# Splitting the first loads by even and odd phases, with direct products ahead of the odd ones, and longer DMA tails in a kernel's own scheduler

## The chip, the cores and the metric

The kernel runs on one core of a Trainium2 chip. The metric is the device time in microseconds (us) of one execution. A profile's span is about 1.8 us shorter than the time of the same execution. Differences between spans are used below to locate time, and differences between timed runs to judge it. Every run quoted here was classed as fast, so no slow run enters a comparison.

Names: TensorE does matmuls and transposes, VectorE and ScalarE do the elementwise work, GpSimd does little here but issue accumulating DMAs, and the sync engine's queue issues nearly all other DMAs.

## The reference, cut to what matters

```python
# B=2, T=4000, D=512, K=5 taps, U=8; all bf16
xp = pad(x, 2)                                     # x (2, 4000, 512)
h  = sum(xp[:, i:i+T, :] @ w1[i] for i in range(5))
h  = gelu(h)[:, ::2, :]                            # stride 2
f  = sum(pad(h, 2)[:, i:i+T1, :] @ w2[i] for i in range(5))
f  = gelu(f)[:, ::2, :]
fe, ge = f @ w_f, g @ w_g
out = tanh(fe[:, :, None, :] + ge[:, None, :, :]) @ w_o   # (2, 1000, 8, 512)
```

## The kernel before

The kernel computes each convolution partly with *direct* products (tap times sample, one output column block) and partly with *transformed* products. In the latter, sums of samples (tiles `xt`) meet sums of taps (tiles `w_t`, `w_b`), so fewer matmuls are needed. The price is work on VectorE, which makes those sums.

A Python object `Plan` records every operation and orders each engine's instructions with a small cost model. In the head, from the first load to the first block of products, the order is pinned to the order of the source on all four engines. After that only TensorE is pinned, and the model decides on the other engines. An engine then runs its instructions in the order that was written.

The part of the model that the change touches tells when a DMA issued by GpSimd is believed to have landed:

```python
HOP = 0.16                                  # us between engines
...
if o.dma and e == "pool":
    soft = max(soft, end + 1.0)
    busy = wire > soft + 1.0
    soft += o.nbytes / (60e3 if busy else 230e3)
    wire += o.nbytes / 220e3 if busy else 0.0
    end = max(soft, end + 2.0)
```

The head loads two pieces of 512 KB (128 partitions with four consecutive samples each, so all four phases), then five taps of `w1` with 512 KB each. It transposes the samples on TensorE, and makes sums:

```python
NWARM = 10
...
def load_xr(rt):                            # all four phases of one piece
    dst = xr[rt][:].map(lambda a: a.rearrange("p r k c -> p (r k c)"))
    src = x[1, 4*P*rt:4*P*(rt+1), :].rearrange("(p r) c -> p (r c)", r=4)
    return pl.dma("sp", lambda e: e.dma_start(dst.ap, src), (), (dst,))
...
came = [load_xr(rt) for rt in range(2)]
came.append(load_w1(0))
for i in (1, 3, 4, 2):
    came.append(load_w1(i, came[-3]))       # issued only when came[-3] has landed
...
warm_mm(NWARM)                              # matmuls of zeros
for pp in range(2):                         # 0: even phases, 1: odd phases
    for rt in range(2):
        ...                                 # 8 transposes on TensorE, then
        if pp: act(o, pv, ACT.Copy)         # eviction on ScalarE
        else:  ...tensor_copy...            # or on VectorE
...
for w in ("b1", "a3"):
    t0.shift(w)                             # ScalarE
for w in ("a0", "a1", "a2", "b3", "b1", "a3"):
    t0.xf(w)                                # VectorE: sums of samples
w1sum13(); w1sums(2, "s"); w1sums(1, "s")   # VectorE: sums of taps
direct(0)                                   # 8 products of the tap w1[0]
filt3("a0")                                 # 12 products
direct(1); direct(3); filt3("b1"); direct(4); filt3("b3", "a3"); direct(2)
pl.pin = ("pe",)
```

## Time and profile before

| | before |
|---|---|
| time, median (range) of 3 runs | 269.05 us (268.66 to 269.43) |
| span of the profiled run | 267.6 us |
| first useful product starts | 7.51 us |
| TensorE's longest wait after its start | 1.64 us, at 57.6 us |

The page's first part for the kernel before gives each engine's busy time, share of the span and instruction count.

```profile
PE 260.0 (97%) x1582; PEld 151.8 (57%) x1582; DVE 201.1 (75%) x362; ACT 181.2 (68%) x302; POOL 6.9 (3%) x20
```

TensorE (PE) is nearly always busy, so a change can gain only by removing TensorE work, by closing its few gaps, or by letting useful products begin sooner. The busy share hides one thing: the first 7.5 us count as busy, but they are zero matmuls and transposes.

This is TensorE's timeline of the kernel before. The columns are start in us, length in us, engine, source line, operation, output and inputs, shapes and count. The bracket gives the idle time before the group and what ended it.

```profile
1.19 4.12 PE L417 MATMUL acc<-zero 128*128 128x512 bf16 x10 [1.19 <-DVE zero L424]
5.15 2.21 PE L510 MATMUL acc<-ident,xr 128*128 128x128 bf16 x32
7.51 1.02 PE L417 MATMUL acc<-xs,w_sb 128*128 128x252 bf16 x8 [0.15 <-issue]
8.37 1.45 PE L417 MATMUL acc<-xt,w_sb 128*128 128x252 bf16 x12
...
16.98 1.45 PE L417 MATMUL acc<-xs,w_t 128*128 128x252 bf16 x12
18.27 2.74 PE L417 MATMUL acc<-xt,w_t 128*128 128x252 bf16 x24
...
23.10 1.15 PE L417 MATMUL acc<-xs,w_t 128*128 128x252 bf16 x8 [0.36 <-issue]
...
59.20 0.60 PE L417 MATMUL acc<-wide,w_t 128*128 128x334 bf16 x3 [1.64 <-DVE wide L404]
```

The eight products at 7.51 are `direct(0)` and the twelve at 8.37 are `filt3("a0")`. The 24 at 18.27 use the summed taps `w_t` that VectorE makes. Starts are what to compare: 12 products from 8.37 to the next group at 9.66 are 1.29 us, 0.1075 us each. The wait at 59.20 is the second convolution's operand `wide`.

What feeds `wide` is visible in ScalarE's timeline of the kernel before (same columns):

```profile
51.07 1.06 ACT L409 ACTIVATE w_t<-half 128x1024 bf16<-128x1024 f32 x1 [1.57 <-DMA half<-w_t]
52.03 0.57 ACT L409 ACTIVATE hT<-acc 128x498 bf16<-128x498 f32 x1
...
54.13 1.06 ACT L409 ACTIVATE w_t<-half 128x1024 bf16<-128x1024 f32 x1 [1.01 <-DMA half<-w_t]
55.09 0.57 ACT L409 ACTIVATE hT<-acc 128x498 bf16<-128x498 f32 x1
```

Twice ScalarE stands and waits for an accumulating DMA into `half` (1.57 and 1.01 us), and an `hT` eviction, from which `wide` is made, stands behind it in the same queue. The model believed that those DMAs had landed already.

The sync queue's timeline of the kernel before shows the loads of the head (start, length of the issuing stretch, waits included):

```profile
0.74 0.87 SPq L440 DMA_DIRECT2D xr<-in_x_dram  x2
1.66 7.63 SPq L435 DMA_DIRECT2D w_sb<-in_w_dram  x5
```

Two whole pieces take 0.87 us to issue, 0.43 us each. The first tap goes out at 1.66. In the table by stretches (start and end, length, busy us of PE, PEld, DVE, ACT and POOL with counts, clock, DMA share, GB/s), the wire is full:

```profile
7.50:10.00 2.50, 2.49 (x24) 2.26 (x25) 2.19 (x5) 2.47 (x4) 0.00 (x0) 1.00 1.02 325
```

### The profile page before, as it was taken

To read this page: it belongs to the slowest core of one execution; us is meant where nothing else is said; L and a number is where in the kernel's file an instruction comes from. 1 tells how busy PE (TensorE), PEld (TensorE's weight loads), DVE (VectorE), ACT (ScalarE), POOL (GpSimd) and SP (SyncE) were. 2 spreads that over 40 slices of the span, in tenths; PEclk is the share of its full clock that TensorE was granted. 3 is DMA by queue.
4 is the path that set the end of the run, shared out by engine and by line. 5 is a ranking of instruction groups with operands and counts; after the bars stand their busy time and mean duration, and the time that the engine had idled before them with its cause. 6 is when DMAs were issued, how large, how long until landed. Compare 5 with 4: busy or idle time off the path is not lost.

```text
span 267.6 us, 4331 instructions
## 1 busy us (share of the span) xinstructions
PE 260.0 (97%) x1582; PEld 151.8 (57%) x1582; DVE 201.1 (75%) x362; ACT 181.2 (68%) x302; POOL 6.9 (3%) x20
## 2 busy tenths in 40 slices
PE   8999999979999899999999999999999999999995
PEld 4897754436666555655655555565564444444442
DVE  1999999889999999994424999743255666666654
ACT  2888969784366999658548488548447695959720
POOL 1000005100000000000000000000000000000000
PEclk9999999999999999999999999999999999999999
DMA  7999998979992022111111214312101443554443
GB/s 244 323 179 218 317 218 152 163 132 198 211 193 48 15 90 72 60 40 60 43 56 39 81 40 138 120 59 78 42 20 60 150 146 118 174 179 160 154 146 131
DMA packets 56706, 33.91 MB, mean 127 GB/s; under 512 B 31582, under 2 KB 56430, under 8 KB 56686
## 3 DMA queue, kind: packets, MB, share of 16 engines
q1 hardware_dynamic: 54430, 31.49, 43.8%
q0 software_dynamic: 2112, 2.10, 4.5%
q8 instruction: 12, 0.20, 0.3%
q10 hardware_dynamic: 144, 0.07, 0.1%
q14 instruction: 8, 0.07, 0.1%
HBM read 7.86 MB, written 16.38 MB: 91 GB/s over the span
## 4 chain that ended last, share of the span: by engine, by line
PE 76%; DVE 16%; issue 3%; DMA 2%; ACT 1%; SPq 0%; DVEq 0%; ACTq 0%
PE acc L417 76%; DVE wide L404 2%; DVE r L585 2%; DMA xr<-in_x_dram 2%; DVE r32b L585 2%; DVE ws L404 2%; DVE hT L404 1%; DVE ws L585 1%; ACT jT L409 1%; DVE w_sb L404 1%; DVE feT L981 1%; DVE w_t L404 1%; DVE sd L585 1%; DVE sd L404 1%; DVE wide L734 1%
## 5 line engine op out<-in xcount | busy, mean ns | idle before, releaser
L417 PE MATMUL acc<-wo_sb,jT 128*128 128x512 bf16 (+1 forms) x504 | 114.9, 377 | 0.7 <-ACT jT L409 0.7
L1029 DVE CAST ost<-acc 128x512 bf16<-128x512 f32 (+1 forms) x95 | 64.7, 686 | 37.9 <-PE acc L417 37.8
L409 ACT ACTIVATE jT<-feT,geT 128x1000 bf16<-128x1000 f32 (+16 forms) x100 | 76.6, 823 | 13.4 <-PE acc L417 10.3
L417 PEld LDWEIGHTS acc<-wo_sb,jT 128*128 128x128 bf16 x504 | 49.2, 98 | 53.5 <-ACT jT L409 1.0
L409 ACT ACTIVATE ost<-acc 128x512 bf16<-128x512 f32 (+1 forms) x31 | 18.1, 584 | 15.9 <-PE acc L417 15.6
L417 PE MATMUL acc<-xt,w_sb 128*128 128x252 bf16 (+1 forms) x144 | 23.5, 305 | 0.0
L409 ACT ACTIVATE hT<-acc 128x334 bf16<-128x334 f32 (+3 forms) x33 | 15.1, 463 | 9.6 <-PE acc L417 9.5
L409 ACT ACTIVATE sd<-acc 128x334 f32<-128x334 f32 (+1 forms) x32 | 14.0, 447 | 11.0 <-PE acc L417 11.0
L417 PE MATMUL acc<-row,w_sb 128*128 128x334 bf16 (+1 forms) x112 | 20.5, 305 | 0.0
L417 PEld LDWEIGHTS acc<-xt,w_sb 128*128 128x128 bf16 x144 | 14.0, 98 | 6.8
L417 PE MATMUL acc<-zx,w_sb 128*128 128x334 bf16 (+1 forms) x96 | 17.6, 305 | 0.0
L404 DVE TENSOR_TENSOR sd<-sd 128x334 f32<-128x334 f32 (+1 forms) x16 | 8.0, 502 | 10.8 <-ACT sd L409 10.7
L417 PE MATMUL acc<-row,w_t 128*128 128x334 bf16 (+1 forms) x80 | 14.6, 305 | 0.0
L417 PEld LDWEIGHTS acc<-row,w_sb 128*128 128x128 bf16 x112 | 10.9, 98 | 6.2
L417 PE MATMUL acc<-xs,w_t 128*128 128x252 bf16 (+1 forms) x76 | 14.0, 314 | 0.4 <-issue 0.4
L417 PE MATMUL acc<-fT,wf_sb 128*128 128x333 bf16 (+1 forms) x96 | 14.0, 305 | 0.2 <-ACT fT L409 0.2
L409 ACT ACTIVATE fT<-acc 128x334 bf16<-128x334 f32 (+1 forms) x16 | 7.1, 447 | 7.9 <-PE acc L417 7.7
L417 PEld LDWEIGHTS acc<-zx,w_sb 128*128 128x128 bf16 x96 | 9.4, 98 | 5.4
L417 PEld LDWEIGHTS acc<-fT,wf_sb 128*128 128x128 bf16 x96 | 9.3, 97 | 4.5 <-ACT fT L409 0.2
L417 PE MATMUL acc<-hT,w_t 128*128 128x334 bf16 x64 | 11.7, 305 | 0.0
L981 DVE COPY feT<-acc 128x334 f32<-128x334 f32 (+1 forms) x16 | 9.2, 608 | 3.2 <-PE acc L417 3.2
L417 PE MATMUL acc<-hT,w_sb 128*128 128x334 bf16 x64 | 11.5, 305 | 0.0
(86 smaller groups left out, 321.1 us busy)
## 6 DMA issues: line engine op xcount, KB each, us to landing
out_dram<-ost SPq DMA_DIRECT2D x109, 128.0 KB, 1.9
w_sb<-in_w_dram SPq DMA_DIRECT2D x10, 512.0 KB, 5.8
xr<-in_x_dram SPq DMA_DIRECT2D x2, 512.0 KB, 4.2
half<-w_sb POOLq DMA_DIRECT2D x2, 512.0 KB, 6.6
half<-w_t POOLq DMA_DIRECT2D x2, 512.0 KB, 5.3
wf_sb<-in_w_f_dram SPq DMA_DIRECT2D x1, 512.0 KB, 6.9
wg_sb<-in_w_g_dram SPq DMA_DIRECT2D x1, 512.0 KB, 5.6
wo_sb<-in_w_o_dram SPq DMA_DIRECT2D x1, 512.0 KB, 6.4
```

The source lines that it names most:

```text
L404: pl.op(eng, lambda e: e.tensor_tensor(out=o.ap, in0=a.ap, in1=b.ap, op=op), (a, b), (o,), vec_cost(o, (a, b)))
L409: pl.op("act", lambda e: e.activation(o.ap, i.ap, func, scale=scale, bias=0.0 if bias is None else bias.ap), rd, (o,), cost or o.ap.free_s ...
L417: ins = e.matmul(o.ap, lhsT=l.ap, rhs=r.ap, start=start and n == 0, stop=stop and n == len(pairs) - 1, skip_group_check=not check)
L585: pl.op(eng, lambda e: e.scalar_tensor_tensor(out=o.ap, in0=a.ap, scalar=f, in1=b.ap, op0=ALU.mult, op1=op), (a, b), (o,), vec_cost(o, (a, ...
L734: pl.op("dve", lambda e: e.scalar_tensor_tensor(out=o.ap, in0=a.ap, scalar=-1.0, in1=b.ap, op0=ALU.mult, op1=sub), (a, b), (o,), vec_cost( ...
L981: pl.op("dve", lambda e, o=o, v=v: e.tensor_copy(out=o.ap, in_=v.ap), (v,), (o,), 0.47)
L1029: pl.op("dve", lambda e, o=o, v=v: e.tensor_copy(out=o.ap, in_=v.ap), (v,), (o,), vec_cost(o, (v,)))
```

## The change

The intent is to start useful products earlier. Each 512 KB piece is split into 256 KB of even phases and 256 KB of odd phases. TensorE begins with `direct(0)` and `a0`, which need only even phases, and transposes the odd ones afterwards. VectorE's and ScalarE's pinned order follows. Three of the ten zero matmuls go. In the scheduler, the modelled DMAs of GpSimd take 2 us longer to land (`tails`).

```diff
-    HOP = 0.16
+    HOP = 0.2
...
-                soft = max(soft, end + 1.0)
+                soft = max(soft, end + 3.0)
...
-                end = max(soft, end + 2.0)
+                end = max(soft, end + 4.0)
...
-    NWARM = 10
+    NWARM = 7
...
-        def load_xr(rt):
-            dst = xr[rt][:]...
-            src = x[1, ...].rearrange("(p r) c -> p (r c)", r=4)
+        def load_xr(rt, pp):
+            dst = xr[rt][pp::2]...
+            src = x[1, ...].rearrange("(p r) c -> p r c", r=4)[:, pp::2, :]
...
-        came = [load_xr(rt) for rt in range(2)]
+        came = [load_xr(rt, 0) for rt in range(2)]
...
         came.append(load_w1(0))
-        for i in (1, 3, 4, 2):
+        came += [load_xr(rt, 1) for rt in range(2)]
+        for i in (4, 1, 3, 2):
             came.append(load_w1(i, came[-3]))
...
-        for pp in range(2):
+        def turn(pp):                       # 16 transposes, 2 evictions
             for rt in range(2):
...
-                if pp:
+                if rt:
                     act(o, pv, ACT.Copy)
...
-        for w in ("b1", "a3"):
-            t0.shift(w)
-        for w in ("a0", "a1", "a2", "b3", "b1", "a3"):
+        turn(0)
+        t0.xf("a0")
+        t0.shift("a3")
+        t0.xf("a3")
+        direct(0)
+        filt3("a0")
+        turn(1)
+        t0.shift("b1")
+        for w in ("b1", "b3", "a1", "a2"):
             t0.xf(w)
         w1sum13()
         w1sums(2, "s")
         w1sums(1, "s")
-        direct(0)
-        filt3("a0")
+        direct(4)
+        filt3("a3")
         direct(1)
         direct(3)
-        filt3("b1")
-        direct(4)
-        filt3("b3", "a3")
+        filt3("b1", "b3")
         direct(2)
```

More of the change, by code (lines that the diff above doesn't have):

```diff
@@ L435, in load_w @@
             return pl.dma(eng, lambda e: e.dma_start(dst.ap, src), (), (dst,))
-        def load_xr(rt):
-            dst = xr[rt][:].map(lambda a: a.rearrange("p r k c -> p (r k c)"))
-            src = x[1, 4 * P * rt:4 * P * (rt + 1), :].rearrange("(p r) c -> p (r c)", r=4)
-            return pl.dma("sp", lambda e: e.dma_start(dst.ap, src), (), (dst,))
+        def load_xr(rt, pp):
+            dst = xr[rt][pp::2].map(lambda a: a.rearrange("p r k c -> p r (k c)"))
+            src = x[1, 4 * P * rt:4 * P * (rt + 1), :].rearrange("(p r) c -> p r c", r=4)[:, pp::2, :]
+            return pl.dma("sp", lambda e: e.dma_start(dst.ap, src), (), (dst,), nbytes=262144)
         def load_x(s, ph, lo, hi):
@@ L501, in bass_standalone__seq2seq_rnn_t_joint__speech_kernel, with fn @@
         psb = ps.h[:, :].bitcast(BF16)
-        for pp in range(2):
+        def turn(pp):
             for rt in range(2):
-                bk = 4 + 2 * pp + rt
+                bk = (1, 3)[rt] if pp else 4 + rt
                 pv = View(psb[:, bk * 1024:(bk + 1) * 1024].rearrange("p (r k c) -> p r k c", r=2, k=NK), np.array([bk]), True)
-                def fn(e, rt=rt, pp=pp, pv=pv):
+                def fn(e, rt=rt, pv=pv):
                     for r in range(2):
@@ L511, in fn @@
                     return ins
-                pl.op("pe", fn, (xr[rt][:], ident[:]), (pv,), 0.8)
+                pl.op("pe", fn, (xr[rt][pp::2], ident[:]), (pv,), 0.6)
                 o = xs[0][pp::2, :, 16 + rt * P:16 + (rt + 1) * P]
-                if pp:
+                if rt:
                     act(o, pv, ACT.Copy)
```

## The prediction

> **What bounds the kernel now.** The page gives a span of 267.6 us and TensorE busy for 260.0 us (97%), the granted clock full in every slice. The list of TensorE waits holds only 1.6 us on VectorE at 57.6 us (the `wide` operands of the second convolution), 1.2 us before the first instruction, 0.7 us on a tanh and 0.5 us of issue. But the head is filler: in the timeline ten zero matmuls run from 1.19 to about 5.2 us and 32 transposes from 4.9 to 7.36 us; the first useful product (`direct(0)`) starts at 7.51 us. The chain of waits starts with 4.6 us on the DMA of `xr` (second piece lands at 5.8 us), runs on TensorE to 37 us, follows VectorE from 37 to 87 us, and is TensorE to the end. VectorE is busy almost without a gap from 7.2 to 52 us, so it is a co-bottleneck.
>
> **What the change does to the head.** Even phases of both pieces need 0.5 MB before the first products instead of 1 MB. At the 367 GB/s of the stretch table for 2.5 to 5 us, 0.5 MB is 1.4 us; I estimate the even pieces at 3.8 and 4.5 us (now 4.4 and 5.8). Seven warm matmuls end near 4.2 us. They start 0.43 us apart, half of full speed; [...]the transposes from 5.15 us run 63 ns apart. The first even transposes may thus still run at half speed. Then the second eviction is on ScalarE (0.97 us, against 0.70 us on VectorE). Sum: `direct(0)` at 6.5 to 7.1 us, 0.4 to 1.0 us earlier.
>
> **What it takes back.** 16 odd transposes (1.0 us at 63 ns) now stand in the middle of the products, no longer hidden before them. The block of 88 products of 0.1075 us ends with `direct(2)` at 16.98 us now; I expect 16.9 to 17.6 us, so nothing is gained there. And VectorE's strict order now holds waits: `a0` for ScalarE's eviction, `a3` for the shift, the odd eviction for the transposes at about 9 us, `b1` for ScalarE's odd eviction and shift (2 x 0.98 us). I estimate 3 to 4 us of idle VectorE before 13 us; the weight sums for `a1`/`a2` (finished by about 19.3 us now) slip by 1 to 2 us, and TensorE waits up to 1.5 us near 20 us. w1 taps land up to 1 us later.
>
> **What the scheduler gives.** Accumulating DMAs from GpSimd are issued for 1.3 us and take 5 to 6.6 us to land (list of issues); the old model expected less. ScalarE stood 1.6 and 1.0 us waiting for them at 49 to 54 us, ahead of the `hT` evictions that VectorE needs for `wide`. Longer tails should move these behind, and remove 0.5 to 1.5 us of the 1.64 us wait at 57.6 us. Everything else is reshuffled by some tenths.
>
> **Sum.** Head -0.7, transposes +1.0, VectorE waits +0.7, scheduler -1.2, and about -0.3 for a change that looks tuned: near -0.5 us. Predicted 268.5 us, 80% range 266.8 to 270.4. Faster by over 2%: 0.02; within 2%: 0.95; slower: 0.03.
>
> **Right or wrong.** Right if `direct(0)` starts 0.4 to 1 us earlier, the odd transposes stand between products, VectorE shows idle between 6 and 13 us, `direct(2)` ends within 0.7 us of 17 us, and the wait before `wide` shrinks. Wrong if the head alone gives over 1 us, if a VectorE backlog raises the waits at 20 or 58 us by over 2 us, if the clock rises a window later (up to +1.7 us), or if the new order changes waits after 90 us.

## The result, and the profile after

| | before | after |
|---|---|---|
| time, median (range), 4 runs each | 269.24 us (268.66 to 269.76) | 272.26 us (271.94 to 273.29) |
| span of the profiled run | 267.6 us | 270.1 us |
| `direct(0)` starts | 7.51 us | 7.93 us |
| products of `acc<-xs,w_t` start | 16.98 us | 19.95 us |
| the eight products after the issue gap start | 23.10 us | 27.52 us |
| wait before `wide` | 1.64 us | none |

The ratio is 1.0119, with a 95% interval of 1.0085 to 1.0154: the change made the kernel 1.2% slower. A ratio here is the mean time of one kernel's fast runs over that of the other's fast runs of the same rounds, so it is not quite the ratio of the medians quoted. The prediction was 268.5 us with a range to 270.4. It was wrong, in the sign of the change too, though the 2% class "same" holds.

TensorE's timeline of the kernel after, in the same columns:

```profile
1.19 3.17 PE L417 MATMUL acc<-zero 128*128 128x512 bf16 x7 [1.19 <-DVE zero L424]
4.15 1.06 PE L511 MATMUL acc<-ident,xr 128*128 128x128 bf16 x8
5.64 0.62 PE L511 MATMUL acc<-ident,xr 128*128 128x128 bf16 x8 [0.42 <-DMA xr<-in_x_dram]
7.93 1.17 PE L417 MATMUL acc<-xs,w_sb 128*128 128x252 bf16 x8 [1.67 <-DMA w_sb<-in_w_dram]
8.89 2.73 PE L417 MATMUL acc<-xt,w_sb 128*128 128x252 bf16 x12
11.41 1.39 PE L511 MATMUL acc<-ident,xr 128*128 128x128 bf16 x16
...
19.95 1.45 PE L417 MATMUL acc<-xs,w_t 128*128 128x252 bf16 x12
22.10 3.20 PE L417 MATMUL acc<-xt,w_t 128*128 128x252 bf16 x24 [0.69 <-DVE w_t L585]
...
27.52 1.15 PE L417 MATMUL acc<-xs,w_t 128*128 128x252 bf16 x8 [0.43 <-issue]
```

Three things stand out. `direct(0)` begins later, not earlier, after 1.67 us of waiting for a *tap*, not for samples. The twelve products at 8.89 last 2.73 us where they lasted 1.45. And the 24 products at 22.10 wait for VectorE's tap sums.

**The balance closes.** All terms are differences of starts in the two timelines:

| term | from | us |
|---|---|---|
| first product later | 7.51 to 7.93 | +0.42 |
| first 20 products | 2.15 us (7.51 to 9.66) against 3.48 (7.93 to 11.41) | +1.33 |
| odd transposes between products | 11.41 to 12.63 | +1.22 |
| the other 68 products up to `acc<-xs,w_t` | 7.32 us in both | 0.00 |
| 12 + 24 + 16 products, waiting for VectorE | 6.12 us (16.98 to 23.10) against 7.57 (19.95 to 27.52) | +1.45 |
| from there to the last product | +4.42 shrinks to +2.56 | -1.86 |
| sum: the last product starts at 264.04 and 266.60 us | | +2.56 |

**The clock.** The table by stretches for the kernel after, over two of the windows in which the clock was recorded (columns as before; the clock is the last but two):

```profile
5.26:8.67 3.41, 1.36 (x15) 1.15 (x16) 1.62 (x3) 2.07 (x2) 0.00 (x0) 1.00 0.73 249
8.68:12.09 3.41, 3.41 (x22) 2.65 (x20) 0.43 (x1) 0.00 (x0) 0.00 (x0) 0.50 0.77 263
```

In the first window TensorE was busy 1.36 of 3.41 us, 40%. In the next window the granted clock was 0.50, so the products there ran at half speed. In the clock records of this run full speed (1.00) stands for 3.41 us, then 0.50 for 3.41 us, then full speed again: these stretches of 3.41 us are called windows below. A window that was 40% busy was followed by half speed. (The expectations quoted below give this half-speed stretch as 8.9 to 12.3 us, and the busy time of the window before it as 1.6 us. That reading was some 0.25 us late; 8.68 to 12.09 and 1.36 us are right.) The odd transposes fall partly into it: they take 1.22 us here and 0.89 us, start to start, at full speed in run `d_whole` below. So the clock cost 1.33 + 0.33 = 1.66 us, and the transposes themselves 0.89.

**The loads.** The sync queue's timeline of the kernel after:

```profile
0.74 1.35 SPq L440 DMA_DIRECT2D xr<-in_x_dram  x2
2.13 0.60 SPq L435 DMA_DIRECT2D w_sb<-in_w_dram  x1
2.78 1.20 SPq L440 DMA_DIRECT2D xr<-in_x_dram  x2
7.70 4.52 SPq L435 DMA_DIRECT2D w_sb<-in_w_dram  x4
```

A 256 KB piece costs 0.60 to 0.68 us to issue (the mean of each pair), more than a whole 512 KB one (0.43). The 512 KB tap behind two pieces took 0.60 us too, and only 0.43 behind two whole loads, so more than the load's own size and pattern enters. So the first tap goes out at 2.13 instead of 1.66. The chain of waits of the kernel after begins with it (start, length, what was waited for):

```profile
2.13 5.55 DMA w_sb<-in_w_dram
```

It lands at 7.68 (7.42 in the kernel before), and `direct(0)` follows 0.25 us later. The samples were hardly earlier. ScalarE's timeline of the kernel after has the eviction of the second even piece, which had landed at 5.59:

```profile
6.29 1.02 ACT L409 ACTIVATE xs<-acc 128x1024 bf16<-128x1024 bf16 x1 [4.06 <-PE acc L511]
```

It ends at 7.31. So even with the tap in place, `direct(0)` could have begun only near 7.4 us (an estimate from these ends and starts), some 0.1 us before the 7.51 of the kernel before.

The next tap is issued only then, because its rule (`came[-3]`) now names the first tap. The wire runs empty meanwhile, as the table by stretches shows for the kernel after, where the kernel before moved 325 GB/s:

```profile
7.50:10.00 2.50, 2.07 (x14) 1.67 (x15) 1.22 (x2) 0.89 (x1) 0.00 (x0) 0.74 0.29 91
```

**VectorE.** Its timeline in the kernel after, the pieces with waits and the tap sums:

```profile
7.35 0.69 DVE L404 TENSOR_TENSOR xt<-xs 128x1008 bf16<-128x1008 bf16 x1 [1.41 <-ACT xs L409]
...
12.39 0.69 DVE L518 COPY xs<-acc 128x1024 bf16<-128x1024 bf16 x1 [3.28 <-PE acc L511]
...
14.97 0.68 DVE L404 TENSOR_TENSOR xt<-xt,xs 128x1008 bf16<-128x1008 bf16 x1 [1.29 <-ACT xt L409]
...
20.22 3.56 DVE L585 SCALAR_TENSOR_TENSOR w_t<-ws,w_sb 128x1024 bf16<-128x1024 f32 x4
```

VectorE stands 3.28 us for the odd transposes, because they come after the first products and VectorE's order has the odd eviction next. The four tap sums end at 23.78 us; in the kernel before, the last that the products at 18.27 needed was done near 19.3 us. TensorE's list of waits for the kernel after shows where that arrives (total us, times, longest):

```profile
PE acc L417 <- DMA w_sb<-in_w_dram: 1.7, 1, 1.7
...
PE acc L417 <- DVE w_t L585: 0.7, 1, 0.7
```

The 1.6 us on `wide` that headed this list before is gone.

### The profile page after: what moved, and what is told of

Same layout as the page of the kernel before. It is cut to its first block, busy times and chain, and to the rows that moved or that the text cites. A ratio compares the mean times of both kernels' runs of the same rounds, so it can differ in the third digit from the quotient of the medians.

```text
span 270.1 us, 4333 instructions
## 1 busy us (share of the span) xinstructions
PE 261.5 (97%) x1579; PEld 152.7 (57%) x1579; DVE 200.9 (74%) x362; ACT 181.1 (67%) x302; POOL 6.8 (3%) x20
## 4 chain that ended last, share of the span: by engine, by line
PE 87%; DMA 5%; DVE 3%; ACT 2%; issue 1%; SPq 0%; ACTq 0%
PE acc L417 87%; DMA w_sb<-in_w_dram 5%; ACT jT L409 1%; DVE w_t L585 1%; DVE feT L985 1%; DVE ws L404 1%; SPq L440 0%; DVE zx L404 0%; DVE w_t L404 0%; ACT w_sb L409 0%; DVE row L734 0%; ACT feT L409 0%; ACT fT L409 0%; ACT ost L409 0%; ACTq L271 0%
## 5 line engine op out<-in xcount | busy, mean ns | idle before, releaser
L417 PE MATMUL acc<-xt,w_sb 128*128 128x252 bf16 (+1 forms) x144 | 24.6, 317 | 0.0
L417 PEld LDWEIGHTS acc<-xt,w_sb 128*128 128x128 bf16 x144 | 14.6, 102 | 7.5 <-DVE xt L404 0.3
L417 PE MATMUL acc<-xs,w_sb 128*128 128x252 bf16 (+1 forms) x72 | 11.5, 296 | 1.7 <-DMA w_sb<-in_w_dram 1.7
```

Source lines behind the costliest of these rows:

```text
L417: ins = e.matmul(o.ap, lhsT=l.ap, rhs=r.ap, start=start and n == 0, stop=stop and n == len(pairs) - 1, skip_group_check=not check)
```

## The experiments

All kernels computed the right result. Medians are of four runs, one of them profiled. Runs of one call share a chip and the runs of the kernel before; its medians were 269.46 us in the first call and 269.29 to 269.39 in the others. The theories:

- **Clock.** The gap before `direct(0)` lets the clock fall, which costs 1.66 us.
- **Order.** Putting 16 transposes between the products costs TensorE 0.9 us and makes VectorE late.
- **Loads.** The finer pieces delay the taps. This is the rival for the late VectorE: it might be starved by late taps and not by its order.
- **Tails.** The scheduler's new numbers give back 1.5 to 1.9 us, by themselves.

| run | median us (range) | ratio to before (95%) |
|---|---|---|
| after | 272.26 (271.94 to 273.29) | 1.0119 (1.0085 to 1.0154) |
| a_sched_only | 267.71 (267.33 to 268.43) | 0.9939 (0.9912 to 0.9965) |
| b_head_only | 273.54 (272.92 to 274.38) | 1.0154 (1.0125 to 1.0183) |
| c_filler | 270.75 (270.27 to 272.07) | 1.0065 (1.0029 to 1.0100) |
| d_whole | 271.65 (270.33 to 273.13) | 1.0083 (1.0040 to 1.0127) |
| e_early_taps | 270.34 (270.19 to 271.26) | 1.0026 (0.9998 to 1.0053) |
| f_sums_first | 270.75 (269.84 to 271.08) | 1.0038 (1.0007 to 1.0068) |
| g_front | 268.02 (267.94 to 268.09) | 0.9942 (0.9919 to 0.9964) |
| h_warm10 | 270.61 (270.46 to 271.27) | 1.0043 (1.0017 to 1.0068) |
| i_sums_first2 | 269.80 (269.59 to 270.08) | 1.0005 (0.9978 to 1.0032) |
| j_pieces_front | 269.71 (269.01 to 272.26) | 1.0022 (0.9968 to 1.0076) |
| k_fill2 | 270.35 (269.84 to 270.64) | 1.0026 (1.0001 to 1.0051) |
| l_tails_only | 267.74 (267.57 to 268.16) | 0.9936 (0.9908 to 0.9965) |
| m_mended | 269.53 (269.11 to 270.05) | 1.0004 (0.9975 to 1.0033) |
| n_tap_first | 272.68 (269.85 to 272.76) | 1.0089 (1.0029 to 1.0148) |

### The two halves of the change

`a_sched_only` is the kernel before with the scheduler's numbers alone; `b_head_only` is the kernel after with the old numbers.

```diff
# a, on before (b: the reverse, on after)
-    HOP = 0.16
+    HOP = 0.2
-                soft = max(soft, end + 1.0)
+                soft = max(soft, end + 3.0)
-                end = max(soft, end + 2.0)
+                end = max(soft, end + 4.0)
```

> The kernel before with only the three scheduler constants of the change (hop 0.2, longer tails of the accumulating DMAs), head untouched. My theory (the head costs, the scheduler gives back): the 1.64 us TensorE wait for the second convolution's operands near 57 us shrinks to under 0.3 us, since ScalarE takes the hT evictions ahead of the DMA-fed copies; 267.2 to 268.2 us, 1.0 to 1.8 us under before. Rival (the new order of the other engines is what costs): 271 us or more. Second rival (constants are neutral): 269.0 to 269.5 us.

> The changed kernel with the old scheduler constants. My theory: the whole loss of the head, about 4.4 us at TensorE's first tanh-eviction wait, shows without the scheduler's gift: 273 to 274.5 us, with a wait of 1 to 1.7 us before the second convolution. Rival (the constants are what costs): 269 us or less.

Measured: 267.71 us for `a`, with no wait before `wide`, and 273.54 us for `b`, with 0.8 us of it. Both times are inside what was expected; the wait in `b` is shorter than the 1 to 1.7 us expected. The scheduler half gains 0.6% and the head half loses 1.5%. The change is a good part and a bad part.

The two halves do not simply add up. From the eight products after the issue gap to the last product (differences of starts), TensorE needs 240.94 us in the kernel before, 240.18 in `b` and 239.08 in the kernel after. So 0.76 of the 1.86 us that the balance gives back is slack which takes up a late head without the new numbers, and these add 1.10. On the kernel before they save 1.77 (239.17 us in `l_tails_only`, below).

`l_tails_only` separates the tails from `HOP`:

```diff
# on before, HOP stays 0.16
-                soft = max(soft, end + 1.0)
+                soft = max(soft, end + 3.0)
-                end = max(soft, end + 2.0)
+                end = max(soft, end + 4.0)
```

> The kernel before with the longer tails of the accumulating DMAs only, hop left at 0.16; TensorE's order is that of before. If the tails give the gain (ScalarE takes the hT evictions ahead of the DMA-fed copies): 267.3 to 268.3 us, the wait before the second convolution under 0.4 us. If the hop gives it: 269 to 269.6 us.

Measured: 267.74 us, the same as `a` within noise. The mechanism is visible in ScalarE's timeline of `l_tails_only`:

```profile
50.00 0.59 ACT L409 ACTIVATE hT<-acc 128x498 bf16<-128x498 f32 x1
...
52.52 0.59 ACT L409 ACTIVATE hT<-acc 128x498 bf16<-128x498 f32 x1 [0.38 <-PE acc L417]
...
53.52 1.05 ACT L409 ACTIVATE w_t<-half 128x1024 bf16<-128x1024 f32 x1
```

The `hT` eviction that ran at 52.03 behind a waiting instruction now runs at 50.00, the next one at 52.52 instead of 55.09, and `w_t<-half` comes after both and waits for nothing. TensorE's `wide` products start at 57.40 instead of 59.20, without a wait. Nothing on TensorE was reordered: only the believed landing time of a DMA.

### The clock

`c_filler` keeps TensorE busy in the gap, `h_warm10` puts the three zero matmuls back at the start, `k_fill2` adds only two in the gap.

```diff
# c: on after
 turn(0)
+warm_mm(7)
# k: on after
 turn(0)
+warm_mm(2)
# h: on after
-    NWARM = 7
+    NWARM = 10
```

> The changed kernel with seven zero matmuls (about 1.5 us at full clock) between the even transposes and the first products, where TensorE idles 1.67 us. My theory: the clock record shows no half-speed stretch from 8.9 to 12.3 us, the 20 first products take 2.15 us instead of 3.5 us, the odd transposes and everything that VectorE hangs on them come 1.3 us earlier: 270.6 to 271.2 us. Rival (TensorE's slow stretch is hidden, because VectorE's weight sums follow the landing of the last w1 tap at 16.1 us): 272 us, unchanged.

> The changed kernel with ten warm matmuls instead of seven; all other engines' orders are the same. If the idle stretch before the first product slows the clock: a half-speed stretch stays in the clock record in most runs, 271.8 to 273 us. If the three missing warm matmuls do: 270.6 to 271.2 us and no half-speed stretch.

> The changed kernel with two zero matmuls (0.4 us) between the even transposes and the first products; the engines' orders are as in the changed kernel. In the traces so far the clock fell after a 3.41 us window in which TensorE was busy 1.6 us, and not after one in which it was busy 1.8 us, with equal idle gaps. If the share of busy time in a window decides (limit near half): no half-speed stretch, 270.5 to 271.2 us. If an idle gap of over a microsecond decides by itself: a half-speed stretch as in the changed kernel, 272 us.

Measured: 270.75, 270.61 and 270.35 us, some 1.5 to 1.9 us under the 272.26 of the kernel after, close to the 1.66 read from the trace. (The kernel after was timed in another call; the medians of the kernel before differ by up to 0.22 us between the calls.) None shows a half-speed stretch after full speed was first granted, and the first 20 products take 2.15 us again in `c` and `k`. `k` needed only 0.59 us of zero matmuls; its window was busy 2.32 of 3.41 us.

The expectation of `h_warm10` named two branches. The idle gap stayed (1.57 us, against 1.67 in the kernel after), and the clock did not fall; the branch of the missing zero matmuls was right. The table by stretches for `h_warm10`, over its window that holds the gap:

```profile
5.84:9.25 3.41, 1.84 (x25) 1.60 (x23) 1.77 (x3) 2.07 (x2) 0.00 (x0) 1.00 0.75 220
```

This window was busy 1.84 us, 54%, and the clock stayed full in the next. In `b_head_only` a window with 1.22 us, 36%, was followed by half speed. The kernel before has a window, on the same 3.41 us grid, that holds its 1.64 us wait for `wide`:

```profile
56.04:59.45 3.41, 1.77 (x10) 0.69 (x8) 2.65 (x8) 3.29 (x8) 0.00 (x0) 1.00 1.01 199
```

It was busy 52%, and full speed stayed in the next. So the busy share of a fixed window fits all these runs, with a limit between 40% and 52%. A limit on the length of a gap is not strictly excluded, but it would have to lie between the 1.64 us that kept the clock and the 1.67 that lost it. The transposes count as busy: this is the first full-speed window of `g_front` (below), for the instructions on `ident`, which are the transposes alone (columns: length, busy PE, PEld and POOL, clock, DMA share, GB/s):

```profile
4.14:7.55 3.41, 2.13 (x32) 1.79 (x32) 0.00 (x0) 1.00 1.05 370
```

All other TensorE work in this window is 0.21 us, and the clock stayed full after it. The zero matmuls of the kernel before thus had a second job which the change took away: not only to bring the clock up (full from 4.84 us there), but to fill the window up to the first product (4.84 to 8.26 us, busy 3.18 us).

### The loads and the order

`d_whole` is the kernel after with whole 512 KB loads, so the order of the change stays and its pieces go. `g_front` is `d_whole` with all transposes ahead of the first product.

```diff
# d: on after
-def load_xr(rt, pp): ...        # 256 KB pieces
+def load_xr(rt): ...            # as in before
-came = [load_xr(rt, 0) for rt in range(2)]
+came = [load_xr(rt) for rt in range(2)]
-came += [load_xr(rt, 1) for rt in range(2)]
# g: on d
+turn(1)
 direct(0)
 filt3("a0")
-turn(1)
```

> The changed kernel with whole 512 KB loads as before and the old distances of the w1 waits, but the new order of transposes and products and the new constants. Pieces theory (splitting is what costs, through late w1 taps): the first product no later than 7.6 us, no hole in the DMA between 8 and 10 us, 270 us or less. Order theory (odd transposes in the middle and the VectorE wait behind them cost): within 1 us of the changed kernel, 271 to 272.5 us.

> The run with whole loads, with the odd transposes put before the first products, where TensorE idles 1.1 us anyway. Theory (transposes in the middle cost 1.06 us on TensorE and start the b1 chain 2.5 us late on VectorE; the idle gap also slows the clock): 267.5 to 268.7 us, no wait near 20 us, runs within 1 us of each other. Rival (the split of the evictions over two engines and the new order of the products cost): 270 us or more.

Measured: `d_whole` 271.65 us, though its profiled run, 270.33 us, was the fastest of the four. The others were not profiled. The one at 271.71 had a mean clock of 0.994, like the kernel after, so it probably had a half-speed stretch; the two at 271.58 and 273.13 had 1.00, and why they were slower is not known. The readings below are those of the profiled run. TensorE's timeline of `d_whole` in its profiled run:

```profile
9.80 1.06 PE L510 MATMUL acc<-ident,xr 128*128 128x128 bf16 x16
...
20.48 3.20 PE L417 MATMUL acc<-xt,w_t 128*128 128x252 bf16 x24 [1.02 <-DVE w_t L584]
```

The wire had no hole here (337 GB/s from 6.16 to 9.57 us), and the first tap landed at 7.14. Yet TensorE still waits 1.02 us for VectorE's tap sums. So the lateness of VectorE comes mainly with the order and not with late taps. `g_front` checks it from the other side. TensorE's timeline of `g_front`:

```profile
7.52 1.02 PE L417 MATMUL acc<-xs,w_sb 128*128 128x252 bf16 x8 [0.27 <-ACT xs L409]
...
18.32 2.98 PE L417 MATMUL acc<-xt,w_t 128*128 128x252 bf16 x24
```

The first product starts at 7.52, hardly before the 7.64 of `d_whole` even though 16 more transposes precede it: they had stood in time in which TensorE was waiting anyway. The wait before the 24 products is gone. `g_front` took 268.02 us, within what was expected. Between the two profiled runs (spans 268.5 and 266.2) lie 2.3 us: the transposes' 0.89 us (start to start), the wait of 1.02, and 0.4 unassigned.

`e_early_taps` is `c_filler` with the taps issued earlier, so that the wire has no hole:

```diff
# on c
-            came.append(load_w1(i, came[-3]))
+            came.append(load_w1(i, came[-5]))
```

> The run with the seven filler matmuls, but the waits of the last four w1 loads set two loads further back (the fourth tap waits for the first x piece instead of for the first tap), so that the DMA hole from 8 to 10 us closes; every engine's order is unchanged. VectorE theory (the weight sums, chained behind the odd transposes, end the wait near 22 us): TensorE's 0.71 us wait for the tap at 11.8 us goes, but the products of the sums start no more than 0.4 us earlier: 270.3 to 270.9 us, within 0.4 us of the filler run. TensorE theory (each wait of TensorE in the head counts): 0.7 us less, 270.0 us, and the wait near 22 us gone too.

Measured: 270.34 us, 0.41 under `c`, which is within the scatter. The wait for the tap in the middle of the products is gone (0.71 us in `c`), and the wait for VectorE's sums came in its place (0.69 us). This agrees with VectorE as the limit, but weakly: the two kernels were timed in different calls, and the profiled run got its full clock late.

### VectorE's order

`f_sums_first` puts the tap sums' first step ahead of waits in VectorE's pinned order. `i_sums_first2` also keeps another tap sum, `w_b`, behind the sums that TensorE needs first.

```diff
# f: on c
 turn(1)
+w1sums(2, "s")
+w1sums(1, "s")
 t0.shift("b1")
...
 w1sum13()
-w1sums(2, "s")
-w1sums(1, "s")
# i: on f, after the last of the four scaled sums is recorded
+scaled = pl.ops[-1]
# and where w_b's sum is recorded:
+pl.ops[-1].after.append(scaled.idx)
```

> The run with the seven filler matmuls, with VectorE's two weight sums (1.8 us, they need only taps that land by 11.6 us) put ahead of the b1 transform that waits for ScalarE. VectorE theory: its idle time between 11.3 and 13.3 us is filled, the last scaled sum is done 0.7 to 1.5 us earlier, 269.4 to 270.2 us. TensorE theory: 270.6 us or more, unchanged or worse because the b1 operands come later.

> The run that put the weight sums first had not tested its point: the scheduler filled the time won with a transform that nobody needs yet (w_b, 1.2 us), just before the scaled sums. Here that transform is held behind them; filler as in the filler run. VectorE theory: the last scaled sum ends near 20.9 us instead of 22.1 us, TensorE does not wait near 21 us, 269.3 to 270.1 us, 0.7 to 1.4 us under the filler run. Rival: unchanged at 270.6 us or more.

`f` was a miss: 270.75 us, exactly the median of `c`. VectorE's timeline of `f_sums_first` says why:

```profile
17.48 1.22 DVE L404 TENSOR_TENSOR w_b<-w_sb 128x2048 bf16<-128x2048 bf16 x1
18.61 3.56 DVE L585 SCALAR_TENSOR_TENSOR w_t<-ws,w_sb 128x512 bf16<-128x512 f32 x4
```

The scheduler put `w_b` (1.22 us) into the time that was won, ahead of the four scaled sums. With `w_b` held back, `i` ran in 269.80 us, 0.95 under `c` (which was timed in another call) and under `f`, and the wait for the sums was gone: the 24 products ran through in 2.59 us, start to start, against 3.01 in `c` and 3.27 in `f`. (In its profile the sums end later than expected, near 21.8 us; that run got its full clock late, at 6.75 us.) So with the clock mended VectorE's lateness was worth between the 0.4 to 0.7 us of these stretches and the 0.95 of the medians, and can be had back without undoing the change's TensorE order. The result is a tie with the kernel before, not a gain.

### Can the idea be made to pay?

Three versions tried to mend everything at once. `j_pieces_front` keeps the four pieces but puts all transposes first, and loads the odd pieces before the first tap. It tells whether the finer pieces alone help; it has the hold of `w_b` from `i`, but neither its filler nor its place of the sums. `m_mended` is `i` with the first tap issued from ScalarE's queue, earlier taps and a shorter filler. `n_tap_first` is `m` with the tap first on the sync queue instead.

```diff
# j: on after, with w_b held back as in i
+came += [load_xr(rt, 1) for rt in range(2)]   # before the first tap
 came.append(load_w1(0))
-for i in (4, 1, 3, 2):
-    came.append(load_w1(i, came[-3]))
+for i, j in ((4, 2), (1, 3), (3, 4), (2, 5)):
+    came.append(load_w1(i, came[j]))
...
+turn(1)                                       # before direct(0), not after filt3("a0")
# m: on i
+came.append(load_w("act", w1_sb[0], ...))     # right after the even pieces
-came.append(load_w1(0))
-    came.append(load_w1(i, came[-3]))
+    came.append(load_w1(i, came[-5]))
-warm_mm(7)
+warm_mm(3)
# n: on m
-came = [load_xr(rt, 0) for rt in range(2)]
-came.append(load_w("act", w1_sb[0], ...))
+came = [load_w("sp", w1_sb[0], ...)]
+came += [load_xr(rt, 0) for rt in range(2)]
```

> The x loads in four 256 KB pieces (even, even, odd, odd, then the first tap), all transposes before the first product as in the run with whole loads and the front order (which gave 268.0 us). If splitting has a price of its own (0.6 to 0.7 us of issue for each piece against 0.4 us for a whole load, a wire less full between 4 and 5.5 us): the first tap lands 0.3 to 0.8 us later than with whole loads and the time is 268.4 to 269.2 us. If splitting is free and only the place of the transposes cost: 267.8 to 268.3 us.

> The change's idea with every found defect of its head mended at once: the first tap is issued from ScalarE's queue at the start beside the x pieces, the later taps two loads earlier, three filler matmuls in the gap, the weight sums ahead of b1, the unneeded transform held back. If the late first tap is an effect of the issue (0.55 to 0.7 us of the sync queue for each piece ahead of it), it lands by 6.5 us and the first product starts near 7.0 us, bound by ScalarE's eviction. If the wire is the cause, it lands at 7.2 us or later. For the whole: if the odd transposes between the products (1.06 us of TensorE) are what the idea cannot get rid of, the time is 268.3 to 269.3 us, still over the 267.7 us of the kernel before with longer tails alone; if the idea pays once mended, 267.3 us or less.

> The mended version again, with the first tap issued first on the sync queue instead of on ScalarE's. In the run before, that tap landed by 5.2 us, [...]the x pieces came last and the first product started at 8.55 us. If the other queue caused that late start: first bytes near 2.5 us again, tap by 4.6 us, even pieces by 5.7 us, first product at 7.0 to 7.5 us, 268.3 to 269.2 us. If it is a late start that any first tap brings: first product after 8 us again and 269.3 us or more. In both cases over the 267.7 us of the kernel before with longer tails, because of the 1.06 us of transposes between the products; under 267.5 us would contradict that.

`j` was expected at 268.4 to 269.2 us and took 269.71 (one of its runs, at 272.26, had a mean clock of 0.987). The four pieces take 2.66 us to issue, so the first tap goes out at 3.44 and lands at 8.71; the first product starts at 8.96, against 7.52 in `g_front`. So pieces that are small here cost 1.4 us at the start and bring nothing.

`m` took 269.53 us, level with the kernel before and just over the 268.3 to 269.3 expected. With the tap on ScalarE's queue, the tap landed first, at 4.75 us (7.68 in the kernel after), but the even pieces landed at 5.50 and 6.23 (3.75 and 5.59 there), and `direct(0)` began at 8.55, not near 7.0. In the trace's DMA records the tap's packets run from 1.84 us, but the first packet of the pieces, issued at the same time, comes only at 3.70 (2.22 in the kernel after). What a second issuing engine gains beyond issuing time, this run does not show cleanly: the even pieces lost, but all five first loads had landed by 7.75 us against 9.02 in the kernel after, with an issue that ended only 0.58 us earlier.

The clock is a second cause in `m` and `n`. TensorE waited for the first piece after only seven zero matmuls (1.18 us in `m`), that window of `m` was busy 2.23 us, and full speed came at 9.54 us. So the even transposes ran at half speed, 16 in 1.89 us. No run tried more zero matmuls there, so these two do not test the order of the loads alone.

`n` was a loss in three of its four runs (272.62 to 272.76 us). TensorE's timeline of `n_tap_first`:

```profile
8.22 1.03 PE L511 MATMUL acc<-ident,xr 128*128 128x128 bf16 x8 [1.57 <-DMA xr<-in_x_dram]
...
10.37 1.86 PE L417 MATMUL acc<-xs,w_sb 128*128 128x252 bf16 x8
```

The tap, issued first, was there at 4.86 us, but the second even piece landed only at about 8.2. The first product started at 10.37, and its eight ran at half speed (1.86 us against 1.02). The two windows with the waits, 2.61 to 6.02 and 6.02 to 9.43 us, were busy 2.16 and 1.83 us, and full speed came only at 12.85 us. One of the four runs took 269.85 us; it was not profiled, and an earlier clock release there is only likely.

A trap for reading: the page gave `n_tap_first` a mean clock of 1.00 and full PEclk digits although those products ran at half speed. The mean is taken from the first clock record on, and before it (5.26 us in the kernel after, 12.85 us in `n_tap_first`) there is none. The length of a known group of matmuls is the safer sign. The slowest runs of the kernel after (273.29 us) and of `b_head_only` (274.38) have a mean clock of 1.00 too; they were not profiled, so a late release there is possible but not shown.

Not settled: why a load that is issued early finishes late when many are in flight, as the second even piece in `n` (near 8.2 us), so that I could not predict landing times to better than a microsecond even after 13 experiments. It also stays open whether some order of these loads could make the idea pay; three mended versions did not get under the kernel before, let alone under the 267.7 us of the tails alone.

**The best kernel** is the kernel before with longer tails (`a_sched_only` or `l_tails_only`), 0.6% faster than the kernel before. It beats both kernels.

## Why the prediction was wrong

| term | predicted us | measured us | shown by |
|---|---|---|---|
| head: `direct(0)` earlier | -0.7 | +0.42 | the two timelines |
| odd transposes between products | +1.0 | +0.89 | timelines; `d_whole` for full speed |
| VectorE late for the tap sums | +0.7 | +1.45 | timelines; `d_whole`, `g_front`, `i_sums_first2` |
| scheduler | -1.2 | -1.86 (-1.10 with the late head, -0.76 slack) | timelines; `a_sched_only`, `b_head_only`, `l_tails_only` |
| "looks tuned" | -0.3 | 0 | no basis |
| clock falls again | 0 (named as a risk, up to +1.7) | +1.66 | records; `c_filler`, `h_warm10`, `k_fill2` |
| sum | -0.5 | +2.56 | spans |

- **The failed step is "`direct(0)` at 6.5 to 7.1 us".** It computed when half of the samples would land, from 0.5 MB and 367 GB/s, and never when the first tap would: its "w1 taps land up to 1 us later" is not set against `direct(0)`, which needs both. The tap had landed at 7.42 us in the kernel before (the profile at hand showed it) and landed at 7.14 in `d_whole`, so with taps issued behind the samples even perfect sample loads could not have brought 6.5. Behind two pieces whose issue took 0.6 to 0.7 us each, it landed at 7.68. The estimate for the samples was off too: 4.5 us for the second even piece, which landed near 5.6, so that its eviction ended only at 7.31. The pages' issue-to-landing times (4.2 us for a 512 KB piece before, where the 367 GB/s used would give 1.4 us, an estimate from these two numbers) already said that bandwidth alone does not set a landing.
- **The clock followed from the same error.** With a gap of 1.67 us and fewer zero matmuls the window dropped to 40% busy. The text had the right size for the loss, but thought of a *later release* and gave a *return* to half speed no weight.
- **The transposes** were sized right.
- **VectorE** was right in mechanism (its order holds waits, 3.28 us before the odd eviction, and the sums for `a1` and `a2` are late). It was under-sized by half: the text's own "TensorE waits up to 1.5 us" was the better figure than the 0.7 in its sum. The runs with whole loads showed that the order, not late taps, makes most of it.
- **The scheduler** was right in mechanism: the whole 1.64 us wait went, not 0.5 to 1.5. Behind the late head the new numbers were worth 1.10 us, close to the 1.2; that later slack would take up another 0.76 of a late head was not foreseen.
- **"Looks tuned" (-0.3)** rested on no number. A change that comes with a tuned look had one part that helped 0.6% and one that hurt 1.5%.

## What to carry to other kernels

When the start of a kernel is to be moved earlier, list every operand of the first useful instruction with its issue time and its measured landing, and move nothing if another operand (here the first tap) lands at the same time as before; filler work that seems idle may be holding up the clock (its fall cost 1.66 us here) and hiding transposes. Work that stood before the last awaited load was free here (the first product of `g_front` starts at 7.52 us, that of `d_whole` at 7.64); the same work moved between the products was paid in full (0.89 us), and the engine that evicts it paid once more in its order (3.28 us of waiting on VectorE). If a scheduler's cost model decides the order, check its DMA landing times against the trace: correcting them was the only part here that gained.

## What the runs show of the clock and the loads

- The return to half speed came after a window that was 40% busy (1.36 of 3.41 us, the kernel after) and in another kernel 36% (1.22 us, `b_head_only`). It did not come after windows with 52% (1.77 us, the kernel before) or more.
- All profiled runs start their first matmul at 1.19 us. Full speed came between 4.14 us (`g_front`) and 7.22 us (`a_sched_only`) in all but two of them, nearly one window (3.41 us) apart. Where TensorE had long waits before (1.18 us in `m_mended`, 1.25 and 1.57 in `n_tap_first`), it came at 9.54 and 12.85 us. Counted back in steps of 3.41 us from the first clock record, a window busy 2.62 us (`a_sched_only`, from 0.39 us) did not bring it, one busy 2.95 us (`g_front`, from 0.72 us) did.
- On the sync engine, issuing a whole 512 KB load took 0.43 us (the kernel before), and a 256 KB piece with a strided pattern 0.60 to 0.68 us (the kernel after): half the bytes cost about half as much again to issue. The 512 KB tap behind two such pieces took 0.60 us.
- From the sync engine, with several loads in flight, the medians from issue to landing were 4.8 us (256 KB pieces, after) and 4.2 to 4.9 us (512 KB loads of the head, before). What sets these times, the runs did not settle.
